# Softmax reciprocals on a spread layout, exponential sums on two engines, and a weight conversion in two parts

## The chip, the cores and the metric

The kernel runs on one core of a Trainium2 chip. A core has a matrix engine (PE, with its own weight loads PEld), a vector engine (DVE), a scalar engine (ACT), a general-purpose engine (POOL) and an engine that issues transfers (SP). Each works through its own queue in order, and semaphores make one wait for another. The metric is the device time of one execution in microseconds (us). The kernel before took 1269.1 us as the median of three runs (1266.14 to 1270.48).

## What is computed

The first half is attention in which a query only sees the keys that fall into its own cluster; the second half is a layer norm followed by a two-layer network with a residual.

```python
q, k, v: (4, 8, 768, 64)      # batch, heads, sequence, head size
q_assign = argmax(q_n @ c_n.T)        # 16 centroids per head, unit vectors
k_assign = argmax(k_n @ c_n.T)
scores = where(q_assign == k_assign, q @ k.T / 8, -1e9)
attn = softmax(scores) @ v            # sum + 1e-9 in the denominator
x = attn laid out as (4, 768, 512)
xn = (x - mean(x)) / sqrt(var(x) + 1e-6) * g_ln
out = x + relu(xn @ w_ch1) @ w_ch2    # 512 -> 2048 -> 512, weights in float64
```

The weights arrive as float64 and are turned into float32 on the chip, by work on their bits.

## The kernel before, in words

**Attention.** Two heads make a pair; there are 16 pairs (4 batches of 4). A pair is worked in two halves of 384 queries each (`g`), and a half in six steps over blocks of 128 keys (`c`). So a pair has 12 steps, a batch 48, and the whole attention 192, numbered `i`. A step computes scores for both heads (`scores`, L297: the cluster mask at L304 and the products at L309 add up in one PSUM tile, ACT takes the exponential at L314 into a tile `e`, four buffers) and, one step later, multiplies them with `v` (`weigh`, L317, into the one accumulator `a_ps`, L324). `weigh` also adds the exponentials up over the six blocks: the add of blocks 0 and 1 is on POOL (L337), the other four are on DVE (L340). Two steps after a half's last block `finish` (L346) sums over the partitions with a matmul against ones (`den_ps`, L353), takes the reciprocal of all 128 x 384 values on DVE (L357; each of the two sums of a query stands there 64 times), multiplies the accumulator with it (L358) into the transposed activations `xT`, and stores two rows of reciprocals in `rdens` (L362) for a range check at the end.

**Preparation.** While a pair is worked, the next one is prepared at its steps 1, 3, 5 and 8: transposes of q and k (L226, copied out at L232 on ACT and L234 on DVE), the nearest centroid (L244 to L267, mostly DVE), and the one-hot masks (L279, copied out at L286 on DVE and L288 on ACT).

**Weights.** `convert_weight` (L171) turns one of 32 chunks of 128 x 512 values into float32: five DVE operations (L180, L183, L187, L188, L192), one on ACT (L194), two on POOL (L195, L196), and for the 16 chunks of the first matrix a scaling on ACT (L198). POOL also issues the load of a chunk (L168). The scratch tiles `raw`, `ta`, `tb` and `low` have two buffers each, so two chunks can be under way. After the 16th chunk `center_w1` (L202) takes the mean of the first matrix out of it (32 matmul records at L207, 16 DVE subtractions at L211). In the written loop a chunk is due at every third step, so the last would come at step 93.

**Network.** `moe_units` (L368) cuts the network of one batch into 62 units: per half 16 `hidden` units (L394, ReLU at L402 into `hT`, 17 buffers) and 12 `project` units (L411, with the residual at L422 and the store at L426), and six `rows` units (transposes L378, copy L381, statistics L383, one square root L387 per batch). From step 96 on one unit is taken per step; what is left runs after the attention.

**Order.** The program is written as one long sequence, but a planner of the framework sets the order of each engine's queue: it takes the earliest written instruction that can start by its own reckoning, and brings later ones forward into idle time of an engine where their buffers are free. So written order and executed order differ, and the number of buffers decides how far a piece of work can be brought forward.

Of the kernel before, what the change touches and what calls it, by code (L numbers as in the profile page):

```python
# [9 lines left out]
F32 = mybir.dt.float32  # L10
# [10 lines left out]
def kernel(  # L21
# [36 lines left out]
    heads = pool("heads", 2)  # L58
    route = pool("route", 2)
    attn = pool("attn", 2)  # L60
    xpool = pool("xpool", 3)
    ps_s = pool("ps_s", 2, space=PSUM)
    ps_a = pool("ps_a", 1, space=PSUM)
    ps_t = pool("ps_t", 3, space=PSUM)
# [38 lines left out]
    nc.gpsimd.memset(eps, 1e-6)  # L103

    onehots = []
    for i in range(2):
        row = []
        for side in "qk":
            oh = const.tile([P, NT, 2, D], BF16, name=f"onehot_{side}{i}")
            nc.gpsimd.memset(oh, 0.0)  # L110
            row.append(oh)
        onehots.append(row)

    rdens = const.tile([B * H * NHALF, HC], F32, name="rdens")


    c_sb = const.tile([H * NCL, D], F32, name="c_sb")
# [53 lines left out]
    def convert_weight(m):  # L171
        _, dst, c = weight_chunk(m)
        words = raws.pop(m).bitcast(U32).rearrange("p (n w) -> p n w", w=2)
        lo, hi = words[:, :, 0], words[:, :, 1]
        cpool = pools["conv"]
        ta = cpool.tile([P, WC], U32, tag="ta", name="ta")
        tb = cpool.tile([P, WC], U32, tag="tb", name="tb")
        fa, fb = ta.bitcast(F32), tb.bitcast(F32)

        nc.vector.tensor_scalar(  # L180
            ta, hi, 0x07FFFFFF, 3, op0=ALU.bitwise_and, op1=ALU.logical_shift_left
        )
        nc.vector.scalar_tensor_tensor(  # L183
            out=ta, in0=hi, scalar=0xC0000000, in1=ta, op0=ALU.bitwise_and, op1=ALU.bitwise_or
        )

        nc.vector.tensor_single_scalar(tb, hi, 0x7FF00000, op=ALU.bitwise_and)  # L187
        nc.vector.scalar_tensor_tensor(  # L188
            out=fa, in0=tb, scalar=float(0x38100000), in1=fa, op0=ALU.is_ge, op1=ALU.mult
        )  # L190

        nc.vector.tensor_single_scalar(tb, ta, 0xFF800000, op=ALU.bitwise_and)  # L192
        low = cpool.tile([P, WC], F32, tag="low", name="low")
        nc.scalar.activation(low, lo, AF.Copy, scale=2.0 ** -52)  # L194
        nc.gpsimd.tensor_tensor(low, low, fb, ALU.mult)  # L195
        nc.gpsimd.tensor_tensor(dst, low, fa, ALU.add)  # L196
        if c is not None:
            nc.scalar.mul(dst, dst, g_sb[:, c : c + 1])  # L198
        if m + 1 == NDC * FF // WC:
            center_w1()  # L200
# [35 lines left out]
    def prep_route(n):  # L236
# [28 lines left out]
        for side, op in ((0, ALU.is_equal), (1, ALU.not_equal)):  # L265
            for j in range(2):
                nc.vector.tensor_tensor(  # L267
                    onehots[n % 2][side][:, :, j, :NCL],
                    revs,
                    first[:, :, side, j].unsqueeze(2).to_broadcast([P, NT, NCL]),  # L270
                    op,
                )

    def prep_onehot(n):
        st = prepared[n]
        for side in range(2):
            t = ps("oh_ps", BF16, 1024)
            for c in range(NT):
                nc.tensor.transpose(  # L279
                    t[:, c * P : (c + 1) * P],  # L280
                    onehots[n % 2][side][:, c, :, :].rearrange("p j d -> p (j d)"),
                    identb,
                )
            m = heads.tile([P, S], BF16, tag=f"m{side}", name=f"m{side}")
            if side == 0:
                nc.vector.tensor_copy(m, t[:, :S])  # L286
            else:
                nc.scalar.mul(m, t[:, :S], -FAR)  # L288
            st["m", side] = m


# [25 lines left out]
    def weigh(i):  # L317
        n, g, c = steps[i]
        e = soft[i]
        if c == 0:  # L320
            accs[n, g] = ps_a.tile([P, 512], F32, tag="a", name="a_ps")
        acc = accs[n, g]
        for j in range(2):
            nc.tensor.matmul(  # L324
                acc[j * D : (j + 1) * D, :HC],
                loaded[n]["v"][:, c, j, :],
                e[:, j, :],
                start=(c == 0),
                stop=(c == NT - 1),
            )  # L330

        if c == 0:
            return
        if c == 1:
            es = attn.tile([P, 2, HC], F32, tag="es", name="es")
            sums[n, g] = es
            nc.gpsimd.tensor_tensor(es, soft.pop(i - 1), e, ALU.add)  # L337
        else:
            es = sums[n, g]
            nc.vector.tensor_tensor(es, es, e, ALU.add)  # L340
        if c > 1:
            soft.pop(i)
        elif c == 1:
            soft.pop(i)

    def finish(n, g):  # L346
        b, pr = pairs[n]
        if b not in x_of:
            x_of[b] = xpool.tile([P, NDC, S], F32, tag="x", name="xT")
        es = sums.pop((n, g))  # L350
        den = ps("den_ps")
        for j in range(2):
            nc.tensor.matmul(  # L353
                den[j * D : (j + 1) * D, :HC], ones, es[:, j, :], start=True, stop=True
            )
        rden = attn.tile([P, HC], F32, tag="rden", name="rden")
        nc.vector.reciprocal(rden, den[:, :HC])  # L357
        nc.vector.tensor_tensor(  # L358
            x_of[b][:, pr, g * HC : (g + 1) * HC], accs.pop((n, g))[:, :HC], rden, ALU.mult
        )  # L360
        r = (n * NHALF + g) * 2
        nc.sync.dma_start(out=rdens[r : r + 2, :], in_=rden[0 : D + 1 : D, :])  # L362


    def ffn():
# [2 lines left out]
    def moe_units(b):  # L368
        xT = x_of[b]
        st = {}  # L370

        def rows(t):
            if t == 0:
                st["x"] = ffn().tile([P, NT, DM], F32, tag="xr", name="xr", bufs=1)
                st["mv"] = small.tile([P, NT, 2], F32, tag="mv", name="mv")
            xp = ps("x_ps")
            for c in range(NDC):
                nc.tensor.transpose(  # L378
                    xp[:, c * P : (c + 1) * P], xT[:, c, t * P : (t + 1) * P], ident
                )  # L380
            nc.scalar.copy(st["x"][:, t, :], xp)  # L381
            bn = small.tile([P, 6], F32, tag="bn", name="bn")
            nc.vector.bn_stats(out=bn, in_=st["x"][:, t, :])  # L383
            nc.vector.bn_aggr(out=st["mv"][:, t, :], in_=bn)
            if t == NT - 1:
                rstd = small.tile([P, NT], F32, tag="rstd", name="rstd")
                nc.scalar.activation(rstd, st["mv"][:, :, 1], AF.Sqrt, bias=eps)  # L387
                nc.vector.reciprocal(rstd, rstd)
                st["rstd"] = rstd

        def hidden(r, f):
            hp = ps("h_ps")
            for c in range(NDC):
# [4 lines left out]
                    start=(c == 0),  # L398
                    stop=(c == NDC - 1),
                )  # L400
            hT = ffn().tile([P, HC], F32, tag="hT", name="hT", bufs=NFC + 1)
            nc.scalar.activation(hT, hp[:, :HC], AF.Relu)  # L402
            st["hT", r, f] = hT

        def project(r, tt, part):
# [12 lines left out]
            if part < NFC // 4 - 1:  # L418
# [1 line left out]
            o = ffn().tile([P, DM], F32, tag="o", name="o_sb", bufs=2)  # L420

            nc.vector.scalar_tensor_tensor(  # L422
                out=o, in0=op, scalar=st["rstd"][:, t : t + 1], in1=st["x"][:, t, :],
                op0=ALU.mult, op1=ALU.add,
            )
            nc.sync.dma_start(  # L426
# [3 lines left out]
        units = []  # L430
        for r in range(NHALF):
            units += [lambda r=r, f=f: hidden(r, f) for f in range(NFC)]
            if r == 0:
                units += [lambda t=t: rows(t) for t in range(NT)]
            units += [
                lambda r=r, tt=tt, p=p: project(r, tt, p)
                for tt in range(TH)
# [15 lines left out]
        prep[s](0)  # L453
    load(1, "qk")
    work = deque()
    conv_ctx = fast.enter_context(ExitStack())
    pools["conv"] = conv_ctx.enter_context(tc.tile_pool(name="conv", bufs=2))
    LAG = 2
    every = LAG * per * NPAIR // NWC
    load_weight(0)  # L460
    scores(0)
    due = {}
    for i in range(len(steps)):
        n, step = divmod(i, per)
        if step == 1 and n + 1 < len(pairs):
            load(n + 1, "v")
        if i in due:
            finish(*due.pop(i))
        if n + 1 < len(pairs) and step in prep:
            prep[step](n + 1)  # L470
            if step == 3 and n + 2 < len(pairs):
                load(n + 2, "qk")
        if i + 1 < len(steps):
            scores(i + 1)
        if i % every == 0 and i // every < NWC:
            m = i // every
            if m + 1 < NWC:
                load_weight(m + 1)
            convert_weight(m)
            if m + 1 == NWC:  # L480
                conv_ctx.close()
                pools["ffn"] = fast.enter_context(tc.tile_pool(name="ffn", bufs=2))
        if i >= LAG * per * NPAIR and work:
            work.popleft()()
        weigh(i)
        _, g, c = steps[i]
        if c == NT - 1:
            if i + 2 < len(steps):
                due[i + 2] = (n, g)
            else:  # L490
                finish(n, g)

        if i % (per * NPAIR) == 3 and i >= per * NPAIR:
            work.extend(moe_units(i // (per * NPAIR) - 1))
    work.extend(moe_units(B - 1))
    while work:
        work.popleft()()
# [2 lines left out]
    def all_in_range():  # L500
        R = rdens.shape[0]
        ends = small.tile([R, 2], F32, tag="ends", name="ends")

        nc.vector.tensor_reduce(ends[:, 0:1], rdens, AX.X, ALU.add)
        nc.vector.tensor_reduce(ends[:, 1:2], rdens, AX.X, ALU.min)
        nc.vector.tensor_single_scalar(ends[:, 0:1], ends[:, 0:1], WIDE, op=ALU.is_le)
        nc.vector.tensor_single_scalar(ends[:, 1:2], ends[:, 1:2], 1.0 / WIDE, op=ALU.is_ge)
        nc.vector.tensor_tensor(ends[:, 0:1], ends[:, 0:1], ends[:, 1:2], ALU.min)
# [205 lines left out]
```

## Time and profile before

One execution was profiled. Its span, first to last instruction, is 1266.0 us, and its own time 1267.76 us; the median of the timed runs is 1269.1 us.

| | us | share of the span |
|---|---|---|
| PE busy | 1178.7 | 93% |
| DVE busy | 462.8 | 37% |
| ACT busy | 294.8 | 23% |
| POOL busy | 173.1 | 14% |
| DVE reciprocals (L357), 32 | 81.7 | |
| DVE adds of exponentials (L340), 128 | 131.0 | |
| POOL adds of exponentials (L337), 32 | 58.0 | |

Busy time is the time in which an engine had an instruction running, including the time in which that instruction was held up. A group's row gives its line, engine and operation, then busy us in total and mean ns of one, then the engine's idle time just before such instructions and what ended it. The share of an engine over the whole span mixes stages with different limits, so a stage is read by itself.

### The profile page before, as it was taken

To read this page: it belongs to the slowest core of one execution; us is meant where nothing else is said; L and a number is where in the kernel's file an instruction comes from. 1 tells how busy PE (TensorE), PEld (TensorE's weight loads), DVE (VectorE), ACT (ScalarE), POOL (GpSimd) and SP (SyncE) were. 2 spreads that over 40 slices of the span, in tenths; PEclk is the share of its full clock that TensorE was granted. 3 is DMA by queue.
4 is the path that set the end of the run, shared out by engine and by line. 5 is a ranking of instruction groups with operands and counts; after the bars stand their busy time and mean duration, and the time that the engine had idled before them with its cause. 6 is when DMAs were issued, how large, how long until landed. Compare 5 with 4: busy or idle time off the path is not lost.

```text
span 1266.0 us, 11625 instructions
## 1 busy us (share of the span) xinstructions
PE 1178.7 (93%) x4738; PEld 561.0 (44%) x4738; DVE 462.8 (37%) x638; ACT 294.8 (23%) x452; POOL 173.1 (14%) x158
## 2 busy tenths in 40 slices
PE   5775778799999999999999999999999999999997
PEld 3332333344444434444434443345455454554553
DVE  6999999755532533232313235220001000010000
ACT  3444322343422331222112223111012010020100
POOL 5566554311101000000000000000000000000000
PEclk9788878999999999999999999999999999999999
DMA  6243242111210110101001000000000000000000
GB/s 171 79 137 92 80 121 67 39 39 38 47 30 13 26 34 21 34 13 25 21 21 34 12 2 1 17 9 1 17 8 1 25 1 8 17 1 17 9 9 19
DMA packets 84188, 42.90 MB, mean 34 GB/s; under 512 B 76896, under 2 KB 76960, under 8 KB 84128
## 3 DMA queue, kind: packets, MB, share of 16 engines
q1 hardware_dynamic: 78848, 25.27, 7.9%
q0 software_dynamic: 4608, 16.78, 4.1%
q8 instruction: 39, 0.64, 0.2%
q14 instruction: 21, 0.17, 0.0%
q10 hardware_dynamic: 672, 0.03, 0.0%
HBM read 35.69 MB, written 6.29 MB: 33 GB/s over the span
## 4 chain that ended last, share of the span: by engine, by line
PE 77%; DVE 5%; issue 1%; ACT 0%
PE h_ps L394 26%; PE o_ps L411 26%; PE a_ps L324 9%; PE s_ps L309 6%; DVE rden L357 3%; PE s_ps L304 2%; PE sim_ps L244 2%; PE den_ps L353 2%; PE qk_ps L226 1%; PE x_ps L378 1%; DVE xT L358 1%; DVE es L340 0%; PE oh_ps L279 0%; DVE w L211 0%; DVE ta L188 0%
## 5 line engine op out<-in xcount | busy, mean ns | idle before, releaser
L394 PE MATMUL h_ps<-xT,w 128*128 128x384 f32 x1024 | 346.7, 493 | 0.0
L411 PE MATMUL o_ps<-w,hT 128*128 128x512 f32 x768 | 341.8, 598 | 0.0
L394 PEld LDWEIGHTS h_ps<-xT,w 128*128 128x128 f32 x1024 | 190.8, 190 | 152.9 <-issue 31.5
L411 PEld LDWEIGHTS o_ps<-w,hT 128*128 128x128 f32 x768 | 142.3, 190 | 185.4 <-issue 184.4
L314 ACT ACTIVATE e<-s_ps 128x768 f32<-128x768 f32 x192 | 154.1, 808 | 293.5 <-PE s_ps L309 291.5
L324 PE MATMUL a_ps<-e,v_sb 128*64 128x384 f32 x768 | 170.8, 542 | 45.7 <-DVE xT L358 28.1
L340 DVE TENSOR_TENSOR es<-es,e 128x768 f32<-128x768 f32 x128 | 131.0, 1024 | 152.8 <-ACT e L314 151.9
L309 PE MATMUL s_ps<-t,t 64*128 64x384 f32 x768 | 168.0, 507 | 0.0
L402 ACT ACTIVATE hT<-h_ps 128x384 f32<-128x384 f32 x128 | 62.7, 490 | 435.7 <-PE h_ps L394 435.7
L422 DVE SCALAR_TENSOR_TENSOR o_sb<-o_ps,rstd,xr 128x512 f32<-128x512 f32 x24 | 18.0, 750 | 330.9 <-PE o_ps L411 330.9
L337 POOL TENSOR_TENSOR es<-e 128x768 f32<-128x768 f32 x32 | 58.0, 1814 | 537.2 <-ACT e L314 537.1
L357 DVE RECIPROCAL rden<-den_ps 128x384 f32<-128x384 f32 x32 | 81.7, 2554 | 134.1 <-PE den_ps L353 134.1
L324 PEld LDWEIGHTS a_ps<-e,v_sb 128*64 128x64 f32 x768 | 44.4, 143 | 159.5 <-issue 92.7
L309 PEld LDWEIGHTS s_ps<-t,t 64*128 64x128 f32 x768 | 74.4, 200 | 4.2 <-issue 4.0
L304 PE MATMUL s_ps<-m,m 64*128 64x384 bf16 x384 | 68.1, 347 | 5.6 <-ACT e L314 5.6
L304 PEld LDWEIGHTS <-m 64*128 64x128 bf16 x384 | 19.4, 94 | 91.0 <-issue 88.4
L195 POOL TENSOR_TENSOR low<-low,tb 128x512 f32<-128x512 f32 x32 | 47.6, 1487 | 48.6 <-DVE tb L192 48.2
L244 PEld LDWEIGHTS sim_ps<-cT,t 128*128 128x128 f32 x384 | 46.6, 201 | 9.2 <-issue 9.2
L244 PE MATMUL sim_ps<-cT,t 128*128 128x32 f32 x384 | 48.4, 285 | 0.0
L383 DVE BATCH_NORM_STATS2 bn<-xr 128x6 f32<-128x512 f32 x24 | 15.8, 679 | 84.2 <-ACT xr L381 84.2
L196 POOL TENSOR_TENSOR w<-low,ta 128x512 f32<-128x512 f32 x32 | 45.1, 1409 | 2.0
L353 PE MATMUL den_ps<-es,ones 128*64 128x384 f32 x128 | 27.9, 515 | 7.0 <-DVE es L340 7.0
(75 smaller groups left out, 492.4 us busy)
## 6 DMA issues: line engine op xcount, KB each, us to landing
raw<-in_moe_w_ch_dram POOLq DMA_DIRECT2D x32, 512.0 KB, 4.1
q_sb<-in_q_dram SPq DMA_DIRECT2D x32, 192.0 KB, 3.1
k_sb<-in_k_dram SPq DMA_DIRECT2D x32, 192.0 KB, 3.3
v_sb<-in_v_dram SPq DMA_DIRECT2D x32, 192.0 KB, 3.2
out_dram<-o_sb SPq DMA_DIRECT2D x24, 256.0 KB, 2.0
rdens<-rden SPq DMA_DIRECT2D x32, 3.0 KB
c_sb<-in_centroids_dram ACTq DMA_DIRECT2D x1, 32.0 KB
g_sb<-in_moe_g_ln_dram ACTq DMA_DIRECT2D x1, 2.0 KB
```

Source lines behind the costliest of these rows:

```text
L244: nc.tensor.matmul(sv[:, c, side, :], st[side][:, c * P : (c + 1) * P], cT[:, pr, :, :].rearrange("p j c -> p (j c)"), start=True, stop=True,)
L304: nc.tensor.matmul(s[:, j, :HC], st["m", 1][rows[j], keys], st["m", 0][rows[j], cols], start=True, stop=False,)
L309: nc.tensor.matmul(s[:, j, :HC], st[1][rows[j], keys], st[0][rows[j], cols], start=False, stop=True,)
L314: nc.scalar.activation(e, s[:, :, :HC], AF.Exp, scale=SCALE)
L324: nc.tensor.matmul(acc[j * D : (j + 1) * D, :HC], loaded[n]["v"][:, c, j, :], e[:, j, :], start=(c == 0), stop=(c == NT - 1),)
L337: nc.gpsimd.tensor_tensor(es, soft.pop(i - 1), e, ALU.add)
L340: nc.vector.tensor_tensor(es, es, e, ALU.add)
L353: nc.tensor.matmul(den[j * D : (j + 1) * D, :HC], ones, es[:, j, :], start=True, stop=True)
L357: nc.vector.reciprocal(rden, den[:, :HC])
L394: nc.tensor.matmul(hp[:, :HC], w1[:, c, f * P : (f + 1) * P], xT[:, c, r * HC : (r + 1) * HC], start=(c == 0), stop=(c == NDC - 1),)
L402: nc.scalar.activation(hT, hp[:, :HC], AF.Relu)
L411: nc.tensor.matmul(op, st["hT", r, f][:, tt * P : (tt + 1) * P], w2[:, f, :], start=(f == 0), stop=(f == NFC - 1),)
```

## The change

- **Reciprocals.** `finish` becomes three parts, due 2, 5 and 9 steps after a half's last block. Part 0: ACT copies the accumulator, not yet divided, into `xT`; the matmul against ones as before; ACT copies one row per head out of PSUM (`dsb`); two transfers spread each row of 384 sums over 64 partitions, six to a partition, in `rdens`. Part 1: DVE takes the reciprocal of 128 x 6 values; a transfer writes them to DRAM, and two more read them back, each row to 64 partitions (`rb`). Part 2: POOL multiplies `xT` with `rb` in place.
- **Sums.** Per half POOL adds blocks 0 and 1 and then block 4; DVE adds blocks 2 and 3, then block 5, then the two part sums. That is two adds on POOL (one before) and three on DVE (four before).
- **Conversion.** `ta`, `tb` and `low` have one buffer instead of two. The first matrix's chunks are due every fourth step (0 to 60), the second's at every step from 64 to 79.
- **Network.** Units start at step 64 instead of 96, at 1.5 per step instead of one; `rows` is split by halves (a square root per half). The scratch of the network no longer waits for that of the conversion.
- **Space.** `xT` has two buffers (three before), the one-hot tiles one set (two), `hT` 16 (17), `xr` half the size.
- The copy of the first one-hot mask moves from DVE to ACT.

```diff
-    xpool = pool("xpool", 3)
+    xpool = pool("xpool", 2)
+    dram = pool("dram", 4, space=bass.MemoryType.DRAM)
...
-    rdens = const.tile([B * H * NHALF, HC], F32, name="rdens")
+    DE = HC // D
+    rdens = const.tile([P, B * NPAIR * NHALF, DE], F32, name="rdens")
...
-        ta = cpool.tile([P, WC], U32, tag="ta", name="ta")
-        tb = cpool.tile([P, WC], U32, tag="tb", name="tb")
+        ta = cpool.tile([P, WC], U32, tag="ta", name="ta", bufs=1)
+        tb = cpool.tile([P, WC], U32, tag="tb", name="tb", bufs=1)
...
-        low = cpool.tile([P, WC], F32, tag="low", name="low")
+        low = cpool.tile([P, WC], F32, tag="low", name="low", bufs=1)
...
-            if side == 0:
-                nc.vector.tensor_copy(m, t[:, :S])
-            else:
-                nc.scalar.mul(m, t[:, :S], -FAR)
+            nc.scalar.mul(m, t[:, :S], -FAR if side else 1.0)
...
+        es = sums.setdefault((n, g), {})
+        if c == 1 or c == 3:
+            es[c] = attn.tile([P, 2, HC], F32, tag=f"es{c}", name=f"es{c}")
+            eng = nc.gpsimd if c == 1 else nc.vector
+            eng.tensor_tensor(es[c], soft.pop(i - 1), soft.pop(i), ALU.add)
+        elif c == 4:
+            nc.gpsimd.tensor_tensor(es[1], es[1], soft.pop(i), ALU.add)
+        elif c == 5:
+            nc.vector.tensor_tensor(es[3], es[3], soft.pop(i), ALU.add)
+            nc.vector.tensor_tensor(es[3], es[3], es[1], ALU.add)
...
+    def finish(n, g, part):
...
+        if part == 0:
...
+            nc.scalar.copy(x_of[b][:, pr, cols], accs.pop((n, g))[:, :HC])
...
+            dsb = attn.tile([P, HC], F32, tag="dsb", name="dsb")
+            nc.scalar.copy(dsb[: D + 1, :], den[: D + 1, :HC])
+            for j in range(2):
+                nc.sync.dma_start(
+                    out=rdens[j * D : (j + 1) * D, r, :],
+                    in_=dsb[j * D : j * D + 1, :],
+                )
+        elif part == 1:
+            nc.vector.reciprocal(rdens[:, r, :], rdens[:, r, :])
+            row = dram.tile([2, HC], F32, tag="row", name="row")
+            nc.sync.dma_start(out=row.rearrange("j (p e) -> (j p) e", e=DE), in_=rdens[:, r, :])
+            rb = attn.tile([P, HC], F32, tag="rb", name="rb")
+            for j in range(2):
+                nc.sync.dma_start(
+                    out=rb[j * D : (j + 1) * D, :],
+                    in_=row[j : j + 1, :].to_broadcast([D, HC]),
+                )
+            late[n, g] = rb
         else:
...
+            x = x_of[b][:, pr, cols]
+            nc.gpsimd.tensor_tensor(x, x, late.pop((n, g)), ALU.mult)
...
-    every = LAG * per * NPAIR // NWC
+    seq = per * NPAIR
+    NW1 = NDC * FF // WC
+
+    begin = {4 * (m % NW1) if m < NW1 else seq + 16 + m - NW1: m for m in range(NWC)}
+    MLP0 = seq + 16
...
+            for part, wait in enumerate((2, 5, 9)):
+                due.setdefault(i + wait, []).append((n, g, part))
+
+        if i >= seq and i % seq == 10:
+            work.extend(moe_units(i // seq - 1))
+        if i >= MLP0:
+            units += 72
+            while work and units >= seq:
+                work.popleft()()
+                units -= seq
+            units = min(units, seq)
```

## The prediction

> **What bounds the kernel now.** The first view is the span in 40 slices of 31.7 us.
>
> ```profile
> PE   5775778799999999999999999999999999999997
> DVE  6999999755532533232313235220001000010000
> POOL 5566554311101000000000000000000000000000
> ```
>
> PE is full from the ninth slice to the end; only the first eight have room, and there DVE is full. Cut at the places where the rows change, in busy us of each engine:
>
> ```profile
> 20.00:233.00 213.00, 151.47 (x764) 67.19 (x762) 203.76 (x264) 75.76 (x111) 124.19 (x102) 0.86 0.34 98
> 233.00:346.50 113.50, 106.78 (x683) 48.49 (x683) 68.95 (x89) 42.85 (x56) 13.58 (x8) 0.97 0.16 36
> 346.50:840.60 494.10, 490.67 (x2073) 217.79 (x2073) 155.24 (x208) 124.31 (x182) 28.89 (x16) 1.00 0.08 20
> 840.60:1258.90 418.30, 418.30 (x1169) 217.80 (x1169) 24.23 (x47) 46.94 (x95) 0.00 (x0) 1.00 0.03 10
> ```
>
> The columns after the length are PE, PEld, DVE, ACT, POOL. Until 233 us DVE is busy 204 of 213 us; after it PE is busy 1016 of 1026. So a gain can only come out of the first 233 us. Network work put earlier in a full PE queue saves nothing. How much is there is seen in one pair during the conversion and one behind it:
>
> ```profile
> 89.56:135.14 45.58, 32.22 (x179) 14.54 (x177) 43.83 (x56) 16.98 (x26) 26.20 (x22) 0.85 0.37 106
> 240.92:269.57 28.65, 26.72 (x178) 12.34 (x176) 17.88 (x23) 11.44 (x16) 3.62 (x2) 1.00 0.19 42
> ```
>
> The same twelve steps take 45.6 us, or 28.65. The order of POOL's queue tells why (start, length, operation):
>
> ```profile
> 226.25 1.32 POOL L195 TENSOR_TENSOR low<-low,tb 128x512 f32<-128x512 f32 x1 [4.09 <-DVE tb L192]
> ...
> 230.89 1.80 POOL L337 TENSOR_TENSOR es<-e 128x768 f32<-128x768 f32 x1
> 232.65 1.27 POOL L196 TENSOR_TENSOR w<-low,ta 128x512 f32<-128x512 f32 x1
> 247.35 1.81 POOL L337 TENSOR_TENSOR es<-e 128x768 f32<-128x768 f32 x1 [13.43 <-ACT e L314]
> ```
>
> The add at 230.89 is the ninth of 32, one per half, so it belongs to step 49, and the last conversion stands beside it. As written, that chunk is due at step 93. The planner has brought all 32 chunks forward into about 51 steps, 1.6 steps per chunk, more than DVE can do beside the attention. The remaining rows are the prices:
>
> ```profile
> L340 DVE TENSOR_TENSOR es<-es,e x128: 894/958/2200, 37.0 to 832.0; 128x768 f32<-128x768 f32 x128
> L357 DVE RECIPROCAL rden<-den_ps 128x384 f32<-128x384 f32 x32 | 81.7, 2554 | 134.1 <-PE den_ps L353 134.1
> L195 POOL TENSOR_TENSOR low<-low,tb x32: 1252/1376/2017, 19.6 to 229.7; 128x512 f32<-128x512 f32 x32
> L337 POOL TENSOR_TENSOR es<-e x32: 1796/1806/1976, 30.1 to 809.3; 128x768 f32<-128x768 f32 x32
> ```
>
> Three numbers after a count are the shortest, median and longest ns. A DVE add of 0.96 us stretches to 2.2 us beside POOL work.
>
> **The change part by part.** I compare by one mark, the exponential of step 64, which started at 267.25 us before; the exponential of step 0 started at 25.92.
>
> Reciprocal: 2.55 us of DVE per half become 0.19 (the 128 x 6 reciprocal of L388 took 0.192 us). The multiply of 0.54 us leaves DVE; POOL gets one of 128 x 384, between half of L337 (0.90 us) and three quarters of L195 (1.03): I take 1.0. ACT gets two copies of 0.48 us (L232's price) per half, and a one-hot copy of 0.81 us per pair (L288's) for DVE's 0.52. ACT was busy 76 of 213 us, so this hides; where ACT stands in a wait for POOL (52 us of L194's waits before) the exponentials queue behind it, and that is in the uncertainty below. The accumulator is now freed by an ACT copy that does not wait for the reciprocal. PE waited 28.1 us for L358 in all, 26.1 of it before 345 us, where DVE was the limit anyway; behind step 64 the part that counts is 6.7 minus what lies before the mark, some 5 us, and 2.0 after 346: I credit 7.
>
> Transfers: SP issues five per half instead of one, four more of 0.54 us (L362), 2.2 us per half of 13 to 32 us. The write to DRAM waits for DVE's reciprocal, the two reads for that write. Loads and output stores queue behind them on SP; q and k have ten steps from load to use and landed in 3.1 to 3.3 us, so they have room. The part steps leave three steps for the first hop and four for the other two, 6.7 and 8.9 us at the fastest pace (2.23 us per step, 26.72 / 12), against landings between 2.0 us (stores) and 4.1 us (weight loads). If the planner places the reciprocal or the POOL multiply too early, DVE or POOL stands with conversions behind it: between 0 and 2 us for each of some eleven halves, 0 to 22 us. I take 0 in the sum, because the steps there run slower than 2.23 us, and keep 22 for the range.
>
> Sums: DVE loses 0.96 us per half, POOL gains 1.81. The last DVE add now waits for POOL's second one, which can sit behind two conversion operations (2.7 us); the matmul against ones, two steps later, waits for that.
>
> Conversion: this decides. With one buffer of `ta`, `tb` and `low` the next chunk's first DVE operation waits for the previous chunk's last POOL operation. The serial chain of a chunk is the five shortest DVE operations, 0.41 + 0.67 + 0.41 + 0.67 + 0.41 = 2.57, and two POOL operations at their medians, 1.38 + 1.33, together 5.3 us. Into it falls other work: per step POOL has (2 x 1.81 + 1.0) / 6 = 0.77 us, DVE (6 x 0.96 + 3.45 routing + 1.06 copies + 0.4) / 12 = 0.89 us. None of it need fall into the chain (0) and all of it may (1.66); a conversion's chain is on DVE half its time and on POOL the other half, so I take about half, 0.9 us per step. A step then lasts 5.3 / r + 0.9, where r is the steps per chunk in the planner's order. The trace shows no order with one buffer. If DVE's time was what held the planner at 1.6 steps, r stays near 1.6; if it was the latency of a chunk, half the buffers double it to 3.2. The written pace is 4. Between 1.6 and 3.2 I take the middle, 2.4: the DVE queue before shows operations of two chunks alternating, with the attention's between, which speaks for both limits. A step is then 5.3 / 2.4 + 0.9 = 3.1 us. `center_w1` cost 18 us (exponentials of steps 46 and 48 at 204.5 and 222.8 us). The mark comes at 25.9 + 64 x 3.1 + 18 = 242 us, 25 us earlier. About five chunks are left at the mark; behind it a step holds 4.2 us or more of network matmuls beside its own 1.7, so they hide. The last `project` part that needs chunk 31 is written into the same step 79 as that chunk; if the cover is gone PE waits one chain, at most 8 us.
>
> This row is where the Trainium skill speaks against the change. By the page SBUF — State Buffer, section Who interferes with whom, a DVE instruction with two SBUF inputs and a GpSimd (POOL) instruction that reads SBUF block each other for the whole instruction. This trace agrees in kind (0.96 us stretched to 2.2). If none of that work overlapped, the POOL 0.77 and the DVE adds of 0.48 us per step would both add to the chain, with the chunk's own 5.3: 3.45 us a step, the mark at 265, and the gain would be 2 us.
>
> Network: the work is the same. A run of units inside a step costs 0.2 us more than in the tail (eight records of L394 2.78 us against 41.28 / 16 = 2.58; L411 3.63 against 3.43). Units now sit in about 122 steps instead of 96: 5 us more. Three more square roots between exponentials bring table loads of 2 x 1.28 us each on ACT, 8 us, hidden where ACT is busy 124 of 494 us. `xT` with two buffers: batch 0's last reader is near step 97, batch 2's first write at 103; without these six steps the write would hold the accumulator.
>
> Sum: -25 (mark) - 7 (accumulator) + 5 (switching) = -27. The profiled execution took 1267.8, so 1241; the median of the runs is 1.3 us above it, so 1242.
>
> **The rivals.** *One chunk at a time is slower (ends slower).* The planner keeps 1.6 steps per chunk, and the queue order forces DVE through 5.3 us of serial chain each: 5.3 / 1.6 + 0.9 = 4.2 us a step for 51 steps, then 13 steps of 2.23: 25.9 + 18 + 215 + 29 = 288, 21 us later; total 1267.8 + 21 - 2 + 1 = 1288. It decides from r below about 1.95 (5.3 / r + 0.9 = 3.5 us gives the old mark, the last 1.6 steps running at PE's pace). For it: DVE was 96% busy, so DVE time may well be the planner's limit. Against it: the planner, too, must wait for the buffers.
> *The written pace holds.* With r = 4 the formula gives 2.23 us a step, PE's own pace; mark at 25.9 + 18 + 143 = 187, 80 us earlier: 1186. Against it: the planner brought chunks forward 42 steps before. At r = 3.2 (2.56 us) the mark is at 208, the total 1208.
> *The gain is eaten.* Half of the work on the two engines blocks the other, or eleven waits of 2 us for transfers: 1242 + 22 to 25, about 1266, no change.
>
> **How the numbers follow.** Less than 0.3% (4 us) can't be told from no change here. My forecast (r 2.1 to 3, 1215 to 1262) 0.42; near the written pace (1180 to 1215) 0.14; no change 0.09; slower by the serial chain, with or without late transfers (1273 to 1310) 0.35. So faster 0.56, same 0.09, slower 0.35. The range leaves out 0.08 below 1204 and 0.11 above 1290; the likeliest case alone is 1215 to 1262.
>
> **What would show it.** Right: POOL's last conversion stands beside the add of a half near step 75, POOL conversions never overlap DVE conversions, PE has no idle time behind step 64, which starts near 242 us. The transfers are hidden if no DVE reciprocal and no POOL multiply waits for one. The serial rival shows as the last conversion near step 51 and DVE waiting for POOL at L180; the written pace as the last conversion at step 79. Wrong beyond that: PE idle behind step 64.

## The result: no change

The changed kernel took 1268.95 us (median; 1267.28 to 1270.19) against 1268.43 us for the kernel before, timed beside it. The ratio is 1.0004 with a 95% interval of 0.9982 to 1.0025. The profiled execution has a span of 1268.4 us (1266.0 before). I had forecast 1242.

The first view is the span in 40 slices:

```profile
PE   6766876799999999999999999999999999999997
DVE  4776776661021112211202021131202011000010
POOL 4676666631110111001110101021110110000000
```

DVE is no longer full in the first eight slices, behind the first it stands at 6 or 7 tenths; and PE is no fuller there than it was, at 6 to 8 tenths. DVE lost 116 us of busy time (462.8 to 346.5), and PE got no further by it in these slices. By stages (after the length: PE, PEld, DVE, ACT, POOL busy):

```profile
90.35:137.28 46.93, 33.70 (x179) 14.16 (x177) 35.98 (x49) 20.28 (x32) 31.02 (x25) 0.82 0.39 102
20.00:263.00 243.00, 181.93 (x901) 80.40 (x899) 173.97 (x244) 97.81 (x151) 157.13 (x121) 0.80 0.36 96
283.00:1261.00 978.00, 978.00 (x3723) 466.56 (x3719) 150.08 (x269) 240.56 (x383) 101.75 (x66) 1.00 0.09 22
```

The first row is one pair, from one routing matmul to the next. Its twelve steps take 46.9 us, as slow as the 45.6 of before, with DVE free for 11 of them and POOL for 16. No engine is full, so something goes round between them. The second row is the conversion; its last operation now ends at 265 us instead of 234. The third says that behind it PE never stands still.

The order of POOL's queue at the end of the conversion:

```profile
258.68 1.27 POOL L194 TENSOR_TENSOR low<-low,tb 128x512 f32<-128x512 f32 x1 [3.26 <-ACT e L310]
259.91 2.52 POOL L334 TENSOR_TENSOR es<-es,e 128x768 f32<-128x768 f32 x1
262.39 0.99 POOL L377 TENSOR_TENSOR xT<-xT,rb 128x384 f32<-128x384 f32 x1
263.34 1.98 POOL L195 TENSOR_TENSOR w<-low,ta 128x512 f32<-128x512 f32 x1
265.29 1.81 POOL L332 TENSOR_TENSOR es<-e 128x768 f32<-128x768 f32 x1
```

L332 at 265.29 is a first add (blocks 0 and 1), the eleventh, that of step 61. So the planner has again brought all 32 chunks forward, by POOL's queue into the first 60 steps: 1.9 steps per chunk. My forecast had taken 2.4. The exponential of step 64 starts at 282.95 us; it was at 267.25 before, and I had put it at 242.

From the exponential of step 0 to that of step 64 PE does the same work in both kernels, but for a few records; the first row is before, the second the changed kernel. The last three columns are the granted clock of PE, the share of the DMA engines and GB/s.

```profile
25.92:267.25 241.33, 180.54 (x945) 80.15 (x947) 219.03 (x283) 85.11 (x125) 122.98 (x100) 0.87 0.31 88
25.85:282.95 257.10, 196.14 (x948) 85.54 (x948) 184.59 (x259) 96.41 (x151) 157.47 (x120) 0.81 0.35 92
```

PE stands for 60.8 us in the first and 61.0 in the second. The delay of 15.8 us is therefore all in its busy time, 15.6 us more for the same matmuls, at a granted clock of 0.81 instead of 0.87. Busy time times clock is 157 and 159 us. So the lighter DVE did not shorten PE's waits at all, and the clock is lower.

What goes round is seen in one chunk, first on DVE, then on POOL, then on ACT:

```profile
181.64 0.43 DVE L179 TENSOR_SCALAR ta<-raw 128x512 uint32<-128x512 uint32 x1 [1.16 <-POOL w L195]
181.98 0.95 DVE L332 TENSOR_TENSOR es<-e 128x768 f32<-128x768 f32 x1
182.85 0.55 DVE L233 COPY t<-qk_ps 128x384 f32<-128x384 f32 x1
183.32 0.68 DVE L182 SCALAR_TENSOR_TENSOR ta<-raw,ta 128x512 uint32<-128x512 uint32 x1
184.04 0.69 DVE L187 SCALAR_TENSOR_TENSOR ta<-tb,ta 128x512 f32<-128x512 uint32 x1
184.76 2.51 DVE L191 TENSOR_SCALAR tb<-ta 128x512 uint32<-128x512 uint32 x1
188.71 0.43 DVE L186 TENSOR_SCALAR tb<-raw 128x512 uint32<-128x512 uint32 x1 [1.44 <-POOL low L194]
```

```profile
184.55 0.59 POOL L167 DMA_DIRECT2D raw<-in_moe_w_ch_dram  x1 [2.94 <-ACT e L310]
185.16 1.81 POOL L334 TENSOR_TENSOR es<-es,e 128x768 f32<-128x768 f32 x1
187.41 1.26 POOL L194 TENSOR_TENSOR low<-low,tb 128x512 f32<-128x512 f32 x1 [0.44 <-DVE tb L191]
188.75 1.50 POOL L195 TENSOR_TENSOR w<-low,ta 128x512 f32<-128x512 f32 x1
```

```profile
181.64 0.67 ACT L193 ACTIVATE low<-raw 128x512 f32<-128x512 uint32 x1 [3.29 <-POOL w L195]
190.29 0.68 ACT L193 ACTIVATE low<-raw 128x512 f32<-128x512 uint32 x1 [6.20 <-POOL w L195]
190.88 0.79 ACT L310 ACTIVATE e<-s_ps 128x768 f32<-128x768 f32 x1
191.57 0.47 ACT L350 COPY xT<-a_ps 128x384 f32<-128x384 f32 x1
```

DVE waits for POOL to free `ta`, works its part of the chunk with attention work in between, and is held up in L191 for 2.5 us (0.41 at the shortest) while POOL issues a load and does an add; then POOL does its two operations. Only then may ACT overwrite `low`: it has stood for 6.2 us with the next exponential and the accumulator's copy queued behind it. This chunk takes 8.65 us from one L193 to the next; the mean of all is 7.4. The main waits from 26 to 261 us in total (us, times, longest):

```profile
ACT low L193 <- POOL w L195: 67.4, 15, 7.4
ACT w L197 <- POOL w L195: 56.7, 15, 7.1
PE a_ps L320 <- ACT e L310: 33.7, 18, 4.0
DVE tb L186 <- POOL low L194: 31.6, 20, 3.3
DVE ta L179 <- POOL w L195: 23.2, 21, 2.5
PE a_ps L320 <- ACT xT L350: 17.1, 4, 6.3
POOL xT L377 <- DMA rb<-row: 1.4, 1, 1.4
```

ACT also stands in L197, the scaling of the first matrix's chunks, which waits for the same POOL operation. The last line clears the small transfers in this kernel: they cost POOL 1.4 us in all, and the profile shows no wait of DVE's reciprocals in this stretch.

So the step mark came 15.7 us later, yet the end only 2.4 us in span. Behind the mark the new kernel is 13.3 us faster. From the mark to the last network matmul, before and after:

```profile
267.25:1258.90 991.65, 983.44 (x3723) 469.45 (x3721) 227.30 (x318) 202.17 (x317) 37.92 (x21) 1.00 0.06 17
```

```profile
282.95:1261.00 978.05, 978.05 (x3723) 466.57 (x3721) 150.08 (x269) 240.61 (x383) 101.75 (x66) 1.00 0.09 22
```

PE stood for 8.2 us before and does not now (6.8 us of that were waits of `a_ps` for the division L358). And the same 3723 records take 5.4 us less. No run takes these 5.4 us apart. By an estimate some 1.5 of them are the clock: from 267 to 346.5 us PE was busy 74.5 us at 0.98 before, and now it has 1.00 from the mark on. The network's units also stand in another place: before a unit stood between the scores and the `weigh` of a step, now up to two stand together behind the `weigh`. The same point in PE's queue, before and after:

```profile
673.02 0.81 PE L309 MATMUL s_ps<-t,t 64*128 64x384 f32 x4
673.76 2.85 PE L394 MATMUL h_ps<-xT,w 128*128 128x384 f32 x8
676.54 0.87 PE L324 MATMUL a_ps<-e,v_sb 128*64 128x384 f32 x4
```

```profile
291.56 0.87 PE L320 MATMUL a_ps<-e,v_sb 128*64 128x384 f32 x4
292.36 5.43 PE L410 MATMUL h_ps<-xT,w 128*128 128x384 f32 x16
297.72 0.34 PE L300 MATMUL s_ps<-m,m 64*128 64x384 bf16 x2
```

From start to start one unit took 2.78 us, and two now take 5.36. From the mark to the last exponential PE's queue holds 94 units in 106 stretches before, and 179 in 119 now.

### The profile page after: what moved, and what is told of

The parts are those of the page before. It is cut to its first block, busy times and chain, and to the rows that moved or that the text cites. A ratio compares the mean times of both kernels' runs of the same rounds, so it can differ in the third digit from the quotient of the medians.

```text
span 1268.4 us, 11879 instructions
## 1 busy us (share of the span) xinstructions
PE 1189.1 (94%) x4738; PEld 563.8 (44%) x4738; DVE 346.5 (27%) x562; ACT 344.6 (27%) x544; POOL 267.7 (21%) x220
## 4 chain that ended last, share of the span: by engine, by line
PE 80%; DVE 1%; POOL 0%; issue 0%; ACT 0%; ACTq 0%; POOLq 0%
PE h_ps L410 27%; PE o_ps L427 27%; PE a_ps L320 9%; PE s_ps L305 7%; PE s_ps L300 3%; PE sim_ps L243 2%; PE den_ps L354 1%; PE qk_ps L225 1%; PE mean_ps L206 1%; PE x_ps L394 1%; PE oh_ps L278 1%; DVE tb L191 0%; POOL low L194 0%; DVE es L336 0%; POOL w L195 0%
## 5 line engine op out<-in xcount | busy, mean ns | idle before, releaser
L320 PE MATMUL a_ps<-e,v_sb 128*64 128x384 f32 x768 | 178.5, 545 | 50.8 <-ACT e L310 33.7
L332 POOL TENSOR_TENSOR es<-e 128x768 f32<-128x768 f32 x32 | 58.0, 1811 | 357.5 <-ACT e L310 357.3
L320 PEld LDWEIGHTS a_ps<-e,v_sb 128*64 128x64 f32 x768 | 39.7, 141 | 166.5 <-issue 53.1
L377 POOL TENSOR_TENSOR xT<-xT,rb 128x384 f32<-128x384 f32 x32 | 34.8, 1089 | 242.2 <-DMA rb<-row 241.6
L334 POOL TENSOR_TENSOR es<-es,e 128x768 f32<-128x768 f32 x32 | 58.6, 1833 | 121.6 <-ACT e L310 121.4
L332 DVE TENSOR_TENSOR es<-e 128x768 f32<-128x768 f32 x32 | 40.7, 1272 | 135.3 <-ACT e L310 135.3
L336 DVE TENSOR_TENSOR es<-es,e 128x768 f32<-128x768 f32 x32 | 33.8, 1056 | 118.7 <-ACT e L310 118.5
L243 PEld LDWEIGHTS sim_ps<-cT,t 128*128 128x128 f32 x384 | 53.7, 224 | 6.3 <-issue 3.2
L243 PE MATMUL sim_ps<-cT,t 128*128 128x32 f32 x384 | 53.8, 303 | 0.0
L195 POOL TENSOR_TENSOR w<-low,ta 128x512 f32<-128x512 f32 x32 | 49.3, 1541 | 2.4
L194 POOL TENSOR_TENSOR low<-low,tb 128x512 f32<-128x512 f32 x32 | 44.5, 1391 | 21.5 <-DVE tb L191 15.1
```

What stands on the lines that cost most here:

```text
L243: nc.tensor.matmul(sv[:, c, side, :], st[side][:, c * P : (c + 1) * P], cT[:, pr, :, :].rearrange("p j c -> p (j c)"), start=True, stop=True,)
L320: nc.tensor.matmul(acc[j * D : (j + 1) * D, :HC], loaded[n]["v"][:, c, j, :], e[:, j, :], start=(c == 0), stop=(c == NT - 1),)
L332: eng.tensor_tensor(es[c], soft.pop(i - 1), soft.pop(i), ALU.add)
L334: nc.gpsimd.tensor_tensor(es[1], es[1], soft.pop(i), ALU.add)
```

## The experiments

The first group asks what holds up the attention during the conversion: the place of the conversions in the queues, the single buffer, or the amount of work. The second takes the parts of the change apart. The ratio is always that to the kernel before, timed beside it.

### The conversions held to their written place

```diff
+    last = {}
...
+            with ExitStack() as behind:
+                for ins in last.values():
+                    behind.enter_context(tc.issue_after(ins))
+                convert_weight(m)
```

`last` holds the newest exponential and the newest DVE add that finishes a sum. The edit sets only an order within a queue; nothing is computed otherwise.

> The changed kernel with one thing added: the DVE and ACT operations of a conversion are queued behind the exponential and the DVE add of the step in which the conversion is written, so that the planner can't bring them forward. Theory A (the conversion pulled into the first 60 steps holds up the attention, one serial chain of 5.3 us for 1.9 steps): at 4 steps per chunk a step costs 5.3 / 4 + 1.1 = 2.4 us, the exponential of step 64 comes near 197 us instead of 283, the second matrix's chunks hide behind the network, and the total is 1185 to 1200. Theory B (the DVE and POOL work as such, or the waits for the small transfers, hold up the attention, wherever the conversion stands): step 64 stays near 270 to 285 and the total within 1% of 1269.

Measured: 1220.09 us, ratio 0.962 (0.9592 to 0.9647); step 64 at 217.6 us, 65 earlier than in the changed kernel. Theory A holds and B falls: the same work, with the same single buffers and the same transfers, is 49 us faster when it is spread over 80 steps.

```profile
26.09:213.41 187.32, 164.49 (x926) 70.44 (x928) 129.22 (x181) 87.65 (x134) 103.97 (x78) 0.94 0.34 87
213.41:340.00 126.59, 116.61 (x481) 57.35 (x480) 74.12 (x121) 44.17 (x71) 67.21 (x56) 0.93 0.31 83
```

From the exponential of step 0 to the mark, to be set beside the two rows of the result:

```profile
24.49:217.64 193.15, 170.31 (x958) 72.74 (x958) 131.15 (x186) 90.57 (x138) 103.97 (x78) 0.94 0.34 86
```

Of the 64 us gained against the changed kernel 38 are waits of PE (22.8 us instead of 61.0) and 26 its busy time, at a clock of 0.94 instead of 0.81; busy time times clock is 160 us here too. No run parts the waits from the clock.

The time is above the expected 1185 to 1200 for two reasons: a step of the first 60 took 2.83 us ((195.97 - 26.09) / 60), not 2.4, and in the second row of the view above PE stands for 10 us.

### The same in the kernel before

The same edit in the kernel before, two buffers, one chunk every third step.

> The kernel before with its conversions held to their written place, one every third step, two buffers, the network from step 96 as before. Theory A (bringing the conversions forward is the loss in this kernel too): a step costs about 2.7 us over the first 93 steps, step 96 comes near 300 us instead of 345, total 1215 to 1235. Theory B (the amount of work on DVE, the reciprocals among it, is the loss): no gain beyond 10 us.

Measured: 1229.76 us, ratio 0.9684 (0.9651 to 0.9717); step 96 at 308.8 us (344.8 before). Theory A holds here too. With all its reciprocals the old kernel gains 38 us by order alone; the changed kernel gained 49.

### Two buffers in the changed kernel

```diff
-        ta = cpool.tile([P, WC], U32, tag="ta", name="ta", bufs=1)
+        ta = cpool.tile([P, WC], U32, tag="ta", name="ta")
...
-            es[c] = attn.tile([P, 2, HC], F32, tag=f"es{c}", name=f"es{c}")
+            es[c] = attn.tile([P, 2, HC], F32, tag=f"es{c}", name=f"es{c}", bufs=1 if c == 1 else 2)
```

(`tb` and `low` likewise; `dsb` has one buffer.)

> The changed kernel with ta, tb and low back at two buffers; for space es1 and dsb have one. The queues now hold all 32 conversions in the first 37 steps (58 with one buffer). Theory A (what counts is how many steps the 32 conversions are squeezed into, since PE gets only so many steps done meanwhile): some 5.8 to 6.3 us per chunk, so step 37 near 215 to 230, step 64 near 290 to 308, total 1270 to 1290, no better than with one buffer. Theory C (the single buffer's serial chain is what eats the gain of the lighter DVE work): step 64 earlier than 267 us and the total 1235 to 1255.

Measured: 1262.43 us, ratio 0.9963 (0.9949 to 0.9977); step 64 at 278.7 us. Between the two: the chain of a single buffer costs some 6 us, but most of the loss stays. (The fewer buffers of `es1` and `dsb` are in this number too.) With two buffers a chunk takes 5.8 us ((212.4 - 27.4) / 32) and by ACT's queue is placed after 1.2 steps (37 / 32); with one it takes 7.4 ((263.3 - 25.9) / 32) and is placed after 1.8 (58 / 32). The quicker the chunks go, the fewer steps PE gets done meanwhile.

### One buffer in the kernel before

> The kernel before with one buffer of ta, tb and low and nothing else changed. The queues hold the 32 conversions in 65 steps (47 before). Theory A: one chain at a time with DVE's reciprocals between, 7.5 to 8 us per chunk, the conversion ends near 265 to 280 us at step 65, where the kernel before is at 269: total 1263 to 1285. Theory C: the serial chain alone costs 15 us or more, total above 1283.

Measured: 1272.7 us, ratio 1.0051 (1.0032 to 1.007); step 64 at 268.2 us. Theory A's range; again about 5 us.

### The old finish in the changed kernel

```diff
-        elif part == 1:
-            nc.vector.reciprocal(rdens[:, r, :], rdens[:, r, :])
...
+        rden = attn.tile([P, HC], F32, tag="rden", name="rden")
+        nc.vector.reciprocal(rden, den[:, :HC])
+        nc.vector.tensor_tensor(
+            x_of[b][:, pr, cols], accs.pop((n, g))[:, :HC], rden, ALU.mult
+        )
```

> The changed kernel with the old finish: DVE takes the reciprocal of all 128 x 384 values and multiplies the accumulator, one transfer instead of five. The conversions stand in the queues up to step 62 (58 in the changed kernel). If the reciprocals are on the path (theory R): in the conversion each of about 10 halves gets 2.36 + 0.54 us more on DVE and 1.0 us less on POOL, the accumulator's wait comes back behind step 64 (about 9 us in the kernel before), total 1280 to 1300. If the serial chain hides them (theory A): only the 9 us behind step 64 come back, 1272 to 1282. If the small transfers cost more than the reciprocals saved (theory T): below 1265.

Measured: 1283.27 us, ratio 1.0114 (1.0082 to 1.0146). That is 14 us above the changed kernel, in theory R's range and 1.3 us above A's. The places speak for A: step 64 starts at 284.6 us, only 1.7 later, though the conversion moved as well (its last chunk ends at 290.8 us, behind the mark). Behind the mark it takes 996.9 us instead of 985.5, and there PE stands again:

```profile
284.61:1273.00 988.39, 983.01 (x3728) 468.49 (x3725) 210.09 (x294) 220.07 (x339) 80.93 (x45) 1.00 0.06 17
```

The new finish is worth some 11 us behind the mark, 5.4 of them idle time of PE. Here the units stand as in the changed kernel and PE's busy time is still 983.0 us (with five records more), so their place alone does not explain the 978.1 of the changed kernel. Theory T falls.

### The old division of the sums in the changed kernel

```diff
-        elif c == 4:
-            nc.gpsimd.tensor_tensor(es[1], es[1], soft.pop(i), ALU.add)
...
+        elif c > 1:
+            es = sums[n, g][3]
+            nc.vector.tensor_tensor(es, es, soft.pop(i), ALU.add)
```

> The changed kernel with the old division of the sums: one add on POOL and four on DVE per half, instead of two and three. The conversions then stand in the queues up to step 52 (58 in the changed kernel). Theory A: less POOL work in the chain (1.8 us per half) shortens a chunk from 7.7 to about 6.9 us, but fewer steps get done meanwhile; the two cancel, total 1262 to 1275. Theory S (the move of adds to POOL is what eats the gain): 1245 to 1258.

Measured: 1263.18 us, ratio 0.9951 (0.9934 to 0.9968), 6 us below the changed kernel; within A's range and above S's. The profiled execution took 1258.4 us, 5 below the median; in it step 64 is at 272.5 us and the last chunk ends at 237.9 instead of 265.3. From step 0 to step 64 it takes 250.2 us instead of 257.1.

### The parts with the pace fixed

Under the paced order the parts weigh in without the planner's moves.

> The changed kernel with paced conversions and the old finish (DVE reciprocal of 128 x 384 values, one transfer). At the loose order the old finish cost 14 us. With the pace fixed, DVE gets 2.9 us more per half in the first 64 steps and POOL 1.0 less. If the new finish is worth its time wherever DVE is not waiting for POOL (theory A): 1235 to 1250, that is 15 to 30 us above the paced kernel's 1220. If the reciprocals hide in DVE's slack: 1222 to 1234.

Measured: 1232.15 us, ratio 0.9721 (0.9705 to 0.9736), 12 us above the paced kernel. The lower reading: DVE's slack hides most of the reciprocals before step 64 (222.7 us, 5 later), and 8 us are behind it.

> The changed kernel with paced conversions and the old division of the sums. With the pace fixed, only the work counts: DVE gets 0.96 us more per half, POOL 1.81 less. If POOL is in the serial chain of a chunk (theory A): 2 to 9 us less than the paced kernel's 1220. If DVE is the limit: 3 to 10 us more.

Measured: 1205.19 us, ratio 0.9494 (0.9468 to 0.9521), 15 us below the paced kernel and below my range. Step 64 starts at 202.6 us, 15 earlier. But 4.5 us of these lie ahead of step 0 (19.95 instead of 24.49 us), before any add: PE waited 0.19 us instead of 2.26 for the first keys to land, and the first 24 routing matmuls took 3.05 us instead of 5.17. That leaves 10.5 us from step 0 to step 64 for the sums, about 1 us in each of ten halves, where the POOL add takes 1.81 and DVE's extra work 0.96. PE's waits there fall by 2.7 us and its busy time by 7.7, with the clock at 0.97 instead of 0.94.

> The changed kernel with paced conversions, the first matrix's chunks at every 3.75 steps and the second's over 20 steps (60 to 79) instead of 16. PE was idle 10 us between 232 and 340 us in the paced kernel, where the second matrix's chunks came one per step. If that idle time is a wait for those chunks: 1210 to 1217. If it is something else: 1219 to 1223.

```diff
-    begin = {4 * (m % NW1) if m < NW1 else seq + 16 + m - NW1: m for m in range(NWC)}
+    begin = {15 * m // 4 if m < NW1 else seq + 12 + 5 * (m - NW1) // 4: m for m in range(NWC)}
```

Measured: 1209.04 us, ratio 0.953 (0.9504 to 0.9555), 1 us below the first range. The first reading holds in the main: from the mark to the end it takes 987.7 us instead of 1001.8, with the mark where it was (217.7). But only 4.2 of PE's 10 us in the paced kernel were direct waits for a chunk. Another 5.2 were a wait for a DVE copy (L233) that stood in DVE's queue behind the start of a chunk (L179), and that start waited for POOL, which had itself waited 3.6 us for a row of reciprocals to be read back.

> Paced conversions, the old division of the sums and the spread places of the chunks together. If the 15 us of the old sums and the 11 us of the spread are separate: 1192 to 1198. If both remove the same wait (PE idle behind step 64): 1203 to 1209.

Measured: 1197.86 us, ratio 0.9443 (0.9428 to 0.9458), the fastest of all, 5.6% below both kernels. The two savings add up to 22 of 26 us, so they are nearly separate.

```profile
20.00:210.00 190.00, 169.70 (x973) 73.53 (x972) 136.61 (x205) 93.86 (x142) 91.69 (x74) 0.95 0.36 94
210.00:345.00 135.00, 132.93 (x532) 62.74 (x533) 72.13 (x114) 45.09 (x71) 58.64 (x49) 0.99 0.27 71
345.00:1190.00 845.00, 843.88 (x3182) 403.48 (x3180) 143.31 (x249) 203.35 (x326) 50.89 (x37) 1.00 0.08 21
```

PE is busy 170 of the 190 us from 20 to 210; the other 20 are what is left there.

> As the one before, with the first matrix's chunks at every 3.5 steps and the second's from step 56 at every 1.5 steps. It moves conversion time from behind step 64, where a step has network work, to before it, where a step has none. If 3.75 steps already left room on DVE and POOL there: 1188 to 1196. If the first 64 steps were full: 1198 to 1208.

Measured: 1203.41 us, ratio 0.9491 (0.9471 to 0.9511). This is the second reading: the first 64 steps were full. With a chunk every 3.5 steps step 64 is at 216.5 us, against 211.2 at 3.75 and 202.6 at 4.

The profiles side by side. "Ahead" is the number of exponentials that stand in ACT's queue before the last chunk's first ACT operation.

| | ahead | step 64 at, us | from there to the end, us | median, us |
|---|---|---|---|---|
| before | 47 | 267.3 | 998.8 | 1268.4 |
| changed | 58 | 283.0 | 985.5 | 1269.0 |
| two buffers | 37 | 278.7 | 984.2 | 1262.4 |
| old finish | 62 | 284.6 | 996.9 | 1283.3 |
| old sums | 52 | 272.5 | 984.2 | 1263.2 |
| paced | 81 | 217.6 | 1001.8 | 1220.1 |
| paced, old sums, spread | 80 | 211.2 | 985.1 | 1197.9 |

## Why the prediction was wrong

*What bounds the kernel.* Right for the large part: the runs that are faster gain in the first stage. Too strict as it stands: 13.3 us came from behind the mark, where PE had still waited 8.2. That network work put earlier saves nothing was not tried by itself.

*The conversion: the step that failed.* The term was "Between 1.6 and 3.2 I take the middle, 2.4" for the steps per chunk. It was 1.9. By my own formula that gives 5.3 / 1.9 + 0.9 = 3.7 us a step; measured were 3.86 ((261.28 - 25.85) / 61), so at this point the formula was 0.2 us off and the wrong r was the larger error. The mark came 16 us later, not 25 earlier. I had named 1.95 as the point below which one chunk at a time loses; 5.3 / r + 0.9 = 3.5 gives 2.04, and 1.9 lies below both. A lighter DVE makes the planner place the chunks closer: with two buffers all 32 stand within 37 steps instead of the 47 of before, and one buffer only moves that to 58. Why it places them so, no run shows.

The formula also has no term for PE, and so missed the other half: PE's waits stayed at 61 us, and its own work grew by 15.6 us at the lower clock. At the paced order the formula gives 5.3 / 4 + 0.9 = 2.2 us a step where 2.83 were measured; PE alone was busy 2.45 us of each (147.0 us in 60 steps, at a clock of 0.93). (The step at 222.8 us, from which I took 18 us for `center_w1`, is step 47, not 48.) The rival "one chunk at a time is slower" was right on this stage, but not on the total.

*Accumulator and switching: the second error, the other way.* I credited 7 us for the accumulator and charged 5 for switching. PE lost its whole idle time behind the mark (8.2 us), and its work there fell by 5.4 us instead of rising by 5. Together -13.6 instead of -2. The visits rose from 106 to 119, which is less than I had counted (96 to 122) but the right way; it was their price that was wrong, and how the 5.4 us divide among the clock, the places of the units and the new finish stays open.

*The sums.* I had priced the added POOL work into "0.9 us per step" as half hidden. The old division is 6 us faster in the changed kernel's own order and 15 with the pace fixed, of which the profile gives the sums 10.5 before the mark.

*The transfers.* Right to take 0 in the sum: 1.4 us of waits in the conversion. In the paced kernel POOL waits more for them, 18.4 us in eight waits up to 345 us, one of them ahead of PE's longest wait.

*The reciprocals.* Right that DVE's time falls; wrong that it counts much in the conversion. The new finish is worth 1.7 us before the mark and 11 behind, and with the pace fixed 5 and 8.

*The rivals.* "The gain is eaten" named the time (1266), not the way: I had it by blocking or late transfers, and it went by a slower first stage and a faster second. In parts, from the single undos: the new finish gains some 14 us, the new sums lose 6, the single buffers lose 6. They were undone one by one, so their sum need not be exact. The earlier start of the network and the changes of space were not undone, so what they are worth is not known. That the forecast was only 2% off in time is therefore no merit of its mechanism: losses and gains cancelled. "The written pace holds" was right about where the time lies, and the paced runs reach it in part.

*Blocking between DVE and POOL.* L191 took 0.41 us at the shortest and averaged 1.18 from 20 to 210 us; five times it took 2.5 where POOL's load issue and an add stood back to back, and twice 3.5 where a POOL multiply followed as well. The Trainium skill, SBUF — State Buffer, section Who interferes with whom, holds that a DVE instruction in a two-port mode and a GpSimd (POOL) instruction block each other for the whole instruction, and so does one with two SBUF inputs against a GpSimd instruction that reads SBUF. These rows agree in kind. The bound that I worked out from it, a mark at 265, was nearer than my sum, but still 18 us early.

Left open: the rest of a paced step, 0.38 us of its 2.83 in which PE stands. By the profile these 22.8 us in 60 steps are 14.1 of waits for exponentials, 6.4 for the one-hot tiles of DVE and 2.1 for the sums; no run takes them apart.

## What to carry to other kernels

Where a planner brings background work forward, the number of buffers is a throttle (37 steps with two, 58 with one), but not the written pace; work meant to be spread must be tied to the steps that it belongs beside. Before making an engine lighter, ask what the freed time will be filled with, and compare where in the queue the last piece of background work stands before and after. Work moved from DVE to POOL is not off the path when both share a chain, or block each other. And look at PE's busy time and granted clock as well as its waits: here 16 us were lost with the waits unchanged.

## What was not expected of the hardware

A DVE operation of 0.41 us (L191) lasted 2.5 us five times; each time it started while POOL issued a load (0.59 us), and POOL went straight on to an add (1.81 us). Before, the same operation (then L192) averaged 0.45 us from 20 to 210 us; the first row is the changed kernel, the second the kernel before:

```profile
L191 DVE TENSOR_SCALAR tb<-ta 128x512 uint32<-128x512 uint32 x25 | 29.4, 1176 | 0.6
```

```profile
L192 DVE TENSOR_SCALAR tb<-ta 128x512 uint32<-128x512 uint32 x28 | 12.6, 450 | 0.1
```

Which operation is held up thus depends on which POOL operation the queue puts beside it.

The granted PE clock goes with PE's waits: 0.81 from step 0 to step 64 in the changed kernel, where PE stands for 61 of 257 us, 0.94 in the paced kernel, where it stands for 23 of 193, and 1.00 behind the mark of the changed kernel, where it never stands. In the first two the same matmuls kept PE busy for 196 and 170 us. The sum of the waits alone does not set the clock: the kernel before also stood for 61 us there, at 0.87. What else does, no run here shows.
